# Sums of weights placed right behind the next pair's centroid products in a routed-attention and cosine-router kernel

## The chip, the cores and the metric

The kernel runs on one core of one Trainium2 chip. Its time is the device time of the whole program in microseconds (us), the median of several runs. Beside it stands one profiled execution, from which every duration of a part is read.

## The reference

The program computes two blocks one after the other. The first is an attention over clusters: queries and keys are assigned to the nearest of 16 centroids, and a query sees only keys of its own cluster. The second is a router with eight experts.

```python
q_assign = argmax(einsum('bhsd,hcd->bhsc', q_n, c_n), -1)   # B, H, S, D = 4, 8, 768, 64; 16 centroids
k_assign = argmax(einsum('bhsd,hcd->bhsc', k_n, c_n), -1)
mask = q_assign[:, :, :, None] == k_assign[:, :, None, :]
scores = where(mask, scale * q @ k.T, -1e9)
attn = softmax(scores)
x = (attn @ v) as (3072, 512)
logits = (x / |x|) @ (emb / |emb|).T / tau                  # 8 experts
e = argmax(logits); gate = softmax(logits)[e]
out = gate * (relu(x @ w1[e]) @ w2[e])                      # w1: 512 x 1024, w2: 1024 x 512
```

## The kernel before

**Pairs and turns.** The attention works on 16 pairs n = 0 to 15, each one batch and two heads. A pair has twelve units in two groups of six: a unit is one block of 128 keys against 384 queries of both heads. The main loop takes two units in one turn, so a pair has six turns, `it` = 0 to 5. The first group ends with turn 2, the second with turn 5. A place is written (pair, turn) here, and in the code's table `early` as (batch, pair of the batch, turn).

**The order is written by hand.** [...] In one turn the order is:

1. transfers of `load`: `v` of the next pair, `q` and `k` of the pair three further on (SP), and in eight pairs a megabyte of expert weights (ScalarE's queue);
2. `scores` of the next turn's two units: per unit four matrix products of the cluster numbers `hot` and four of q and k (L454) into `s_ps`, which has two buffers; `expo` (L465, ScalarE) turns them into `prob`, which has five;
3. `between(n, it)`, which holds everything that prepares the next pairs or serves the router, and the table `early` with the first part of the placement of tokens;
4. `attend` of this turn's two units: TensorE multiplies by `v` into `o_ps` (L476), which has one buffer; VectorE adds `prob` into `acc` (L485, L495). At a group's last unit ScalarE copies `o_ps` to `o_sb` (L500). The next group's first L476 must wait for that copy;
5. `unite` (GpSimd adds the halves of `o_sb`, L509), `divide` and `total`.

**Preparing a pair** (`prep_pieces`). `turn0` and `turn1` transpose q and k on VectorE (L356, `qT` and `kT`). `products` multiplies both by the centroids (L366, TensorE, into a `misc` buffer in PSUM, of which there are two), and VectorE transposes that to `asn` (L375). `choose` finds the best centroid on VectorE (L384 to L387: `amax`, `sel` twice, `pm`), writes it into `cd` on ScalarE (L389, L392), and SP transposes `cd` by a transfer into `hot` (L397), which the pair's first scores need, in turn 5 of the pair before.

**Finishing a pair.** `total` sums `acc` over the keys with products by ones (L523, TensorE, into `misc`); VectorE transposes these sums (L540) and takes their reciprocal (L541), GpSimd copies it eight times (L544). `divide` spreads it (L555, `den`) and multiplies (L559, `xT`). `rows` transposes `xT` (L576, `xb`) and SP writes it to `x_rows` in DRAM (four transfers).

**Routing a batch** (`route_pieces`), in the turns of the next batch. `products` multiplies `xT` by the experts (L598), `logits` transposes and adds (L611, L614), `choose` takes the best (L651 to L658), `read` fetches two blocks of `x_rows` back (SP, into `xr`), and `norms` squares and sums one block (L637, ScalarE). `pa.ranks`, `pa.firsts`, `pa.experts`, `pa.dest`, `pa.hot_blocks` and `pa.hot_rows` place the tokens of the first two batches.

**Experts.** After the last pair, 28 blocks of 128 tokens go through `turn_x` (the tokens transposed: by TensorE and an eviction for the first six, L958 and L961, by VectorE for the others, L951), `hidden` (L973, then L980) and `result` (L989, then L999 and L1000).

Of the kernel before, what the change touches and what calls it, by code (L numbers as in the profile page):

```python
# [39 lines left out]
def kernel(  # L40
# [12 lines left out]
    nc = tc.nc  # L53
# [23 lines left out]
    PIECES = KA + 2  # L77
# [77 lines left out]
    NP = len(pairs)  # L155
# [127 lines left out]
    def turned_experts():  # L283
        bk = misc()
        for c in range(KD):
            nc.tensor.transpose(
                bk[:, E * c : E * c + E], emb[:, P * c : P * c + P], ident[0:E, 0:E]
            )
        nc.vector.tensor_copy(
            embT[:, :, 0:E], bk[:, 0 : KD * E].rearrange("p (c e) -> p c e", e=E)  # L290
        )
# [278 lines left out]
    def rows(*gs):  # L570

        n, hq, _ = units[GU * gs[0]]
        b, hp = pairs[n]
        G = len(gs)
        xb = smp.tile([P, G * HS // SQ, SQ], F32, tag="xb", name="xb", bufs=2)
        nc.vector.transpose(  # L576
            xb.rearrange("p g i -> p (g i)"),
            xT[b, hp][:, hq : hq + G].rearrange("p k t -> p (k t)"),
        )
        t0 = S * b + HS * hq  # L580
        for c in range(P // SQ):
            c0 = P * c + SQ * hp
            nc.sync.dma_start(
                out=x_rows[t0 : t0 + G * HS, c0 : c0 + SQ].rearrange("(g t) i -> t g i", t=SQ),
                in_=xb[SQ * c : SQ * c + SQ],
            )
# [395 lines left out]
    def result(j, halves=(0, 1)):  # L982
# [30 lines left out]
    prepare, route = {}, {}  # L1013
    pa = Places(0, rta)
    early = {
        (2, 2, 0): pa.ranks,
        (2, 2, 4): pa.firsts,
        (2, 2, 5): pa.experts,
        (2, 3, 0): lambda: pa.dest(0),
# [13 lines left out]
    def piece(n, name, *args):  # L1033
        if n < NP:
            if n not in prepare:
                prepare[n] = prep_pieces(n)
            prepare[n][name](*args)

    def between(n, it):
        b, nb = divmod(n, NHP)  # L1040
        if n == 0:

            if it == 0:
                piece(1, "turn0")
                piece(1, "turn1")
            elif it == 1:
                piece(1, "products")
            elif it == 2:
                piece(1, "choose")
                turned_experts()  # L1050
        elif it == 0:
            piece(n + 1, "products")
        elif it == 1:
            piece(n + 1, "choose")
        elif it == 3:
            rows(2 * n - 2, 2 * n - 1)
        if it == 4:
            piece(n + 2, "turn0")
        elif it == 5:
            piece(n + 2, "turn1")  # L1060
        if b > 0:
            if nb == 0 and it == 3:
                route[b - 1] = route_pieces(b - 1)
            products, logits, read, norms, choose = route.get(b - 1, (None,) * 5)

            m = NJ * nb + it
            if m in (8, 11, 14):
                read((m - 8) // 3 * 2, (m - 8) // 3 * 2 + 2)
            if m in (11, 12, 14, 15, 17, 18):
                norms((11, 12, 14, 15, 17, 18).index(m))  # L1070
            if (nb, it) == (0, 4):
                products(0)
            elif (nb, it) == (0, 5):
                products(1)
            elif (nb, it) == (1, 2):
                logits(0)
            elif (nb, it) == (1, 3):
                logits(1)
            elif (nb, it) == (1, 4):
                choose()  # L1080
        if n == NP - 1 and it == 4:
            route[b] = route_pieces(b)
            route[b][2](0, NJ, 0, P - SQ)
        if b == B - 1 and (nb, it) == (3, 0):
            for j in range(2):
                weights1(j)
                weights2(j)
# [10 lines left out]
    with tc.manual_schedule(engines=by_hand):  # L1098
        begin()
        for i in range(0, len(units), 2):  # L1100
            n, it = divmod(i // 2, NJ)

            if n == it == 0:
                load(2, "qk")
            if it == 2 and n + 1 < NP:
                load(n + 1, "v")
            if it >= 4 and n + 3 < NP:
                load(n + 3, "qk"[it - 4])
            if it == 3 and n in (1, 2, 3, 5, 6, 7, 9, 10):

                slot, part = divmod(n - 1 - n // 4, 4)
                w, c, x = ((w1s, KD, moe_w1), (w2s, KF, moe_w2))[part // 2]
                cs = slice(c // 2 * (part % 2), c // 2 * (part % 2) + c // 2)
                nc.scalar.dma_start(
                    out=w[slot][:, cs], in_=x[0].rearrange("(c p) f -> p c f", p=P)[:, cs]
                )
            for m in range(i + 2, min(i + 4, len(units))):
                scores(m)
                expo(m)
            between(n, it)  # L1120
            if it == 4 and n == NP - 1:
                divide(2 * n)
            b, nb = divmod(n, NHP)
            if (b, nb, it) in early:
                early[b, nb, it]()
            if i + 2 == len(units):
                ats.close()
                tile_waits = {"side": "right", "reuse_waits": "tile"}
                psX = ctx.enter_context(tc.tile_pool(name="psX", bufs=1, space=PSUM, **tile_waits))
                turn_x(0, nc.scalar.copy, xp.tile([P, DM], F32, tag="acc", name="xTm", bufs=3))  # L1130
            for m in range(i, i + 2):
                attend(m)
            if it == 2:
                if n > 0:
                    divide(2 * n - 2, 2 * n - 1)
                unite(2 * n)
            elif it == 5:
                unite(2 * n + 1)
            if i + 2 == len(units):
                rows(ngroups - 2)  # L1140
                route[b][0](0)
            if it == 0 and n > 0:
                total(2 * n - 2, 2 * n - 1)
            elif it == 3 and n == NP - 1:
                total(2 * n)
        at.close()
        mop = ctx.enter_context(tc.tile_pool(name="mop", bufs=2, **tile_waits))
        rtb = ctx.enter_context(tc.tile_pool(name="rtb", bufs=1, **tile_waits))
        psH = ctx.enter_context(tc.tile_pool(name="psH", bufs=3, space=PSUM, **tile_waits))

        products, logits, read, norms, choose = route[B - 1]
        pb = Places(1, rtb)
        gates = gate_pieces(0, B - 1)
        gates[0]()
        hidden(0, (0,))
        order_x(3)
        total(ngroups - 1)
        divide(ngroups - 1)
        ato.close()
        psY = ctx.enter_context(tc.tile_pool(name="psY", bufs=2, space=PSUM, reuse_waits="tile"))  # L1160
        rows(ngroups - 1)
        gates[1]()
        gates[2]()
        hidden(0, (1,))
        gates[3]()
        weights1(2)
        turn_x(1, nc.scalar.copy)
        logits(0)
        read(0, NJ, P - SQ, P)
        products(1)  # L1170
        hidden(1, (0,))
        logits(1)
        choose()
        hidden(1, (1,))
        weights1(3)
        turn_x(2, nc.scalar.copy)
        pb.ranks()
        pb.firsts()
        for j in range(KA):
            fetch_gate(j)  # L1180
        result(0, (0,))
        pb.dest(0)
        pb.dest(1)
        pb.experts()
        result(0, (1,))
        weights2(2)
        pb.hot_blocks()
        pb.hot_rows(0, 1)
        hidden(2)
        weights1(4)  # L1190
        pb.tokens()
        fetch(4)
        fetch(5)
        for j in range(NJ):
            norms(j)
        gates = gate_pieces(B - 1, B)
        gates[0]()
        result(1, (0,))
        pb.pieces()
        fetch(6)  # L1200
        turn_x(3, nc.scalar.copy)
        for gate in gates[1:3]:
            gate()
        result(1, (1,))
        weights2(3)
        gates[3]()
        order_x(4)
        order_x(5)
        hidden(3)

        for j in range(2, usual):
            if 3 < j + 1 < usual:
                turn_x(j + 1, nc.vector.tensor_copy)
                if j + 4 < usual:
                    fetch(j + 4)
                hidden(j + 1)
                fetch_gate(j + 1)
            if 4 < j + 3 < usual:
                weights1(j + 3)
            result(j)  # L1220
            if 3 < j + 2 < usual:
                weights2(j + 2)

# [63 lines left out]
```

## Time and profile before

| | us |
|---|---|
| median of 3 runs | 758.27 |
| lowest and highest run | 758.07, 760.18 |
| the profiled execution | 759.15 |
| its span, first to last instruction | 757.4 |

The attention ends near 346 us of the span, where the first L973 starts; the rest is the experts' work. The profile page gives each engine's busy time and its share of the span, then groups of instructions: line, engine, operation, tiles, how often, then busy time and mean duration, then the idle time of the engine before them and what ended it. The list of waits gives, for an engine's line and what it waited for, the sum in us, the number of waits and the longest. The timeline gives start, duration and instruction, with the idle time before it in brackets. L12 is line 12 of the kernel before.

### The profile page before, as it was taken

How to read it: one execution, taken by the hardware profiler on the slowest of the kernel's cores; microseconds unless marked ns; L12 is line 12 of the kernel's file. 1: busy time of each engine (PE TensorE's matmuls, PEld its weight loads, DVE VectorE, ACT ScalarE, POOL GpSimd, SP SyncE). 2: the span in 40 equal slices, each digit the busy share in tenths (PEclk: the TensorE clock that was granted, in tenths of full speed). 3: DMA queues.
4: the chain of work that ended last, by engine and by line, in shares of the span. 5: the costliest groups of instructions: out<-in, count | busy, mean ns of one | idle time of the engine just before them, and what ended most of it. 6: DMA issues, size and time to landing. Idle time of an engine off the chain costs nothing. (4 is left out here: it accounts for less than half of the span.)

```text
span 757.4 us, 16422 instructions
## 1 busy us (share of the span) xinstructions
PE 734.9 (97%) x6670; PEld 442.7 (58%) x6670; DVE 328.2 (43%) x522; ACT 275.5 (36%) x438; POOL 253.6 (33%) x367
## 2 busy tenths in 40 slices
PE   7999999999988999999999999999999999999994
PEld 3444444444444444447766776776776776767762
DVE  5788887988769898987510100000000000000000
ACT  4666665766546555764150111111101111111110
POOL 2022222432121232460543453453453443543111
PEclk9999999999999999999999999999999999999998
DMA  9557876987578655487898865999767774147300
GB/s 147 86 115 152 164 124 134 196 163 146 91 165 183 109 95 97 109 268 169 283 367 319 301 238 186 337 331 332 245 236 249 261 252 147 49 148 253 122 15 24
DMA packets 246154, 140.26 MB, mean 185 GB/s; under 512 B 208177, under 2 KB 208177, under 8 KB 246076
## 3 DMA queue, kind: packets, MB, share of 16 engines
q1 hardware_dynamic: 236268, 117.09, 58.6%
q0 software_dynamic: 6432, 13.66, 5.0%
q10 hardware_dynamic: 3376, 8.44, 3.5%
q8 instruction: 54, 0.88, 0.5%
q14 instruction: 24, 0.20, 0.1%
HBM read 158.40 MB, written 13.64 MB: 227 GB/s over the span
## 5 line engine op out<-in xcount | busy, mean ns | idle before, releaser
L973 PEld LDWEIGHTS h_ps<-xTm,w1s 128*128 128x128 f32 x1792 | 204.3, 192 | 16.1 <-issue 12.7
L973 PE MATMUL h_ps<-xTm,w1s 128*128 128x128 f32 x1792 | 205.5, 275 | 2.2 <-DVE xTm L961 1.6
L989 PE MATMUL y_ps<-w2s,hT 128*128 128x512 f32 x448 | 197.0, 593 | 0.0
L465 ACT ACTIVATE prob<-s_ps 128x768 f32<-128x768 f32 x192 | 153.5, 812 | 95.2 <-PE s_ps L454 87.5
L454 PE MATMUL s_ps<-qT,kT 64*64 64x384 f32 x1536 | 156.0, 482 | 0.0
L476 PE MATMUL o_ps<-prob,v 64*64 64x385 f32 x1536 | 145.8, 493 | 5.3 <-ACT o_sb L500 3.3
L989 PEld LDWEIGHTS y_ps<-w2s,hT 128*128 128x128 f32 x448 | 83.0, 190 | 93.7 <-issue 93.7
L951 DVE STREAM_TRANSPOSE xTm<-xin 128x512 f32<-128x512 f32 x22 | 15.6, 711 | 272.9 <-remote 179.6
L495 DVE TENSOR_TENSOR acc<-acc,prob 128x768 f32<-128x768 f32 x128 | 123.7, 967 | 8.1
L980 ACT ACTIVATE hT<-h_ps 128x512 f32<-128x512 f32 x56 | 33.4, 597 | 203.9 <-PE h_ps L973 120.9
L476 PEld LDWEIGHTS o_ps<-prob,v 64*64 64x64 f32 x1536 | 56.9, 134 | 75.5 <-issue 58.3
L889 POOL DMA_INDIRECT xin<-x_rows,pidx x88 | 89.4, 1016 | 30.3 <-issue 28.1
L509 POOL TENSOR_TENSOR o_sum<-o_sb 128x385 f32<-128x385 f32 x30 | 32.2, 1073 | 156.8 <-ACT o_sb L500 156.7
L1000 POOL DMA_INDIRECT out_dram<-y,sidx x24 | 24.6, 1025 | 168.4 <-ACT y L999 162.5
L454 PEld LDWEIGHTS s_ps<-qT,kT 64*64 64x64 f32 x1536 | 56.1, 133 | 38.7 <-issue 35.6
L454 PE MATMUL s_ps<-hot 64*64 64x384 bf16 x768 | 64.7, 325 | 1.8 <-DVE hot L415 1.0
L999 ACT ACTIVATE y<-y_ps,gatein 128x512 f32<-128x512 f32 x28 | 19.2, 687 | 129.4 <-PE y_ps L989 123.2
L544 POOL COPY inv<-inv 32x12 f32<-32x12 f32 x120 | 43.9, 365 | 52.8 <-DVE inv L541 48.5
L454 PEld LDWEIGHTS <-hot 64*64 64x64 bf16 x768 | 23.3, 107 | 38.2 <-issue 36.9
L485 DVE SCALAR_TENSOR_TENSOR acc<-prob,prob 128x768 f32<-128x768 f32 x32 | 31.3, 979 | 0.0
L889 POOL DMA_INDIRECT gatein<-gate_rows,gidx x28 | 28.3, 1010 | 8.9 <-issue 8.9
L500 ACT COPY o_sb<-o_ps 128x770 f32<-128x770 f32 x32 | 25.5, 798 | 14.9 <-PE o_ps L476 14.3
(201 smaller groups left out, 359.1 us busy)
## 6 DMA issues: line engine op xcount, KB each, us to landing
w1s<-in_moe_w_dram SPq DMA_DIRECT2D x28, 2048.0 KB
w2s<-in_moe_w_dram SPq DMA_DIRECT2D x28, 2048.0 KB
v<-in_v_dram SPq DMA_DIRECT2D x128, 48.0 KB
q<-in_q_dram SPq DMA_DIRECT2D x60, 96.0 KB
k<-in_k_dram SPq DMA_DIRECT2D x60, 96.0 KB
x_rows<-xb SPq DMA_DIRECT2D x60, 96.0 KB
xr<-x_rows SPq DMA_DIRECT2D x9, 512.0 KB
w1s<-in_moe_w_dram ACTq DMA_DIRECT2D x4, 1024.0 KB
```

The costliest lines, as they stand in the source:

```text
L454: nc.tensor.matmul(s_ps[D * half : D * half + D, h, 0:HS], lhsT=l[rows, half], rhs=r[rows], start=part == (1 if len(parts) < 2 else 0), st ...
L465: nc.scalar.activation(d["prob"][:, :, 0:HS], d["s_ps"][:, :, 0:HS], ACTF.Exp, scale=scale)
L476: nc.tensor.matmul(g["o_ps"][D * h : D * h + D, half, 0:HE], lhsT=ld[n]["v"][keys, j, h], rhs=d["prob"][keys, h, 0:HE], start=(j == 0), st ...
L485: nc.vector.scalar_tensor_tensor(out=g["acc"], in0=un[i - 1]["prob"][:, :, 0:HS], scalar=NJ * EPS, in1=d["prob"][:, :, 0:HS], op0=ALU.add, ...
L495: nc.vector.tensor_tensor(g["acc"], g["acc"], d["prob"][:, :, 0:HS], ALU.add)
L500: nc.scalar.copy(t["o_sb"], g["o_ps"][:, :, 0:HE])
L509: add(t["o_sum"][:, hq], t["o_sb"][:, 0], t["o_sb"][:, 1], ALU.add)
L544: nc.gpsimd.tensor_copy(inv2[M * to : M * to + M, :, i % 2], inv[M * i : M * i + M])
L889: nc.gpsimd.indirect_dma_start(out=to, out_offset=None, in_=of, in_offset=bass.IndirectOffsetOnAxis(ap=at, axis=0), bounds_check=n - 1, oo ...
L973: nc.tensor.matmul(bk[:, m : m + P], lhsT=w1s[j % 2][:, c, f0 + m : f0 + m + P], rhs=d["xT"][:, P * c : P * c + P], start=(c == 0), stop=( ...
L980: nc.scalar.activation(d["hT"][:, f0 : f0 + 512], bk, ACTF.Relu)
L989: nc.tensor.matmul(bk, lhsT=d["hT"][:, P * c : P * c + P], rhs=w2s[j % 2][:, c], start=(c == 0), stop=(c == KF - 1),)
```

## The change

Five things move; no instruction of the computation is added or dropped.

- `turn0` of the pair after next goes from turn 4 to turn 5, `turn1` from turn 5 to turn 0 of the next pair, `products` from turn 0 to 1, `choose` from turn 1 to 2, `rows` from turn 3 to 4, `divide` from turn 2 to 3, the load of `v` from turn 2 to 0, the weights' transfer from turn 3 to 4. In the last pair `rows`, `divide` and `total` stay.
- `total` of the pair before goes from the end of turn 0 to the middle of turn 1, right behind `products`.
- The router's products, logits and choosing come one turn later; the reads go out in turns 9, 13 and 15 of a batch (before: 8, 11, 14), and the norms come in turns 15, 16, 18, 19, 21, 22 (before: 11, 12, 14, 15, 17, 18).
- `pa.ranks` goes from turn 0 to turn 3 of pair 10.
- Among the experts, `turn_x(1)` comes right behind the last `total`, `turn_x(2)` between the halves of `hidden(1)`, and `turn_x(4)` and `turn_x(5)` between the halves of a result instead of right ahead of the `hidden` that uses them.

```diff
-        (2, 2, 0): pa.ranks,
+        (2, 2, 3): pa.ranks,
...
-        elif it == 0:
-            piece(n + 1, "products")
-        elif it == 1:
-            piece(n + 1, "choose")
-        elif it == 3:
-            rows(2 * n - 2, 2 * n - 1)
-        if it == 4:
+        else:
+            if it == 0:
+                piece(n + 1, "turn1")
+            elif it == 1:
+
+                piece(n + 1, "products")
+                if n + 1 < NP:
+                    total(2 * n - 2, 2 * n - 1)
+            elif it == 2:
+                piece(n + 1, "choose")
+            if it == (4 if n + 1 < NP else 3):
+                rows(2 * n - 2, 2 * n - 1)
+        if it == 5:
             piece(n + 2, "turn0")
-        elif it == 5:
-            piece(n + 2, "turn1")
...
-            if m in (8, 11, 14):
-                read((m - 8) // 3 * 2, (m - 8) // 3 * 2 + 2)
-            if m in (11, 12, 14, 15, 17, 18):
-                norms((11, 12, 14, 15, 17, 18).index(m))
-            if (nb, it) == (0, 4):
+            if m in (9, 13, 15):
+                third = (9, 13, 15).index(m)
+                read(2 * third, 2 * third + 2)
+            if m in (15, 16, 18, 19, 21, 22):
+                norms((15, 16, 18, 19, 21, 22).index(m))
+            if (nb, it) == (0, 5):
                 products(0)
-            elif (nb, it) == (0, 5):
+            elif (nb, it) == (1, 0):
                 products(1)
-            elif (nb, it) == (1, 2):
+            elif (nb, it) == (1, 3):
                 logits(0)
-            elif (nb, it) == (1, 3):
+            elif (nb, it) == (1, 4):
                 logits(1)
-            elif (nb, it) == (1, 4):
+            elif (nb, it) == (1, 5):
                 choose()
...
-            if it == 2 and n + 1 < NP:
+            if it == (0 if n else 2) and n + 1 < NP:
                 load(n + 1, "v")
...
-            if it == 3 and n in (1, 2, 3, 5, 6, 7, 9, 10):
+            if it == 4 and n in (1, 2, 3, 5, 6, 7, 9, 10):
...
+            if n > 0 and it == (3 if n + 1 < NP else 2):
+                divide(2 * n - 2, 2 * n - 1)
             if it == 2:
-                if n > 0:
-                    divide(2 * n - 2, 2 * n - 1)
                 unite(2 * n)
...
-            if it == 0 and n > 0:
+            if it == 0 and n == NP - 1:
                 total(2 * n - 2, 2 * n - 1)
...
         total(ngroups - 1)
+        turn_x(1, nc.scalar.copy)
...
-        turn_x(1, nc.scalar.copy)
...
         choose()
+        turn_x(2, nc.scalar.copy)
         hidden(1, (1,))
         weights1(3)
-        turn_x(2, nc.scalar.copy)
...
             if 3 < j + 1 < usual:
-                turn_x(j + 1, nc.vector.tensor_copy)
+                if j + 1 >= PIECES:
+                    turn_x(j + 1, nc.vector.tensor_copy)
...
-            result(j)
+            result(j, (0,))
+
+            if 3 < j + 2 < PIECES:
+                turn_x(j + 2, nc.vector.tensor_copy)
+            result(j, (1,))
```

## The prediction

> **What bounds the kernel now.** I read four views in this order: the page's busy shares, the waits of TensorE, the timeline around the two slices where TensorE dips, and the timeline of an undisturbed pair.
>
> ```profile
> PE 734.9 (97%) x6670; PEld 442.7 (58%) x6670; DVE 328.2 (43%) x522; ACT 275.5 (36%) x438; POOL 253.6 (33%) x367
> ...
> L476 PE MATMUL o_ps<-prob,v 64*64 64x385 f32 x1536 | 145.8, 493 | 5.3 <-ACT o_sb L500 3.3
> ```
>
> TensorE is the bound; something moves the end only if it shortens TensorE's own stream or a wait in it. Its waits:
>
> ```profile
> PE o_ps L476 <- ACT o_sb L500: 3.3, 2, 2.8
> ...
> PE h_ps L973 <- DVE xTm L961: 1.6, 2, 0.8
> ...
> PE h_ps L973 <- ACT xTm L961: 0.6, 1, 0.6
> ...
> ACT junk L637 <- DMA xr<-x_rows: 10.2, 5, 4.1
> ```
>
> The last line says why the first exists. The norms (L637) stand in ScalarE's queue ahead of the copy of `o_sb` (L500), and `o_ps` has one buffer, so the next group's L476 waits for that copy:
>
> ```profile
> 221.37 0.63 ACT L637 ACTIVATE junk<-xr 128x512 f32<-128x512 f32 x1 [4.14 <-DMA xr<-x_rows]
> ...
> 222.00 0.78 ACT L500 COPY o_sb<-o_ps 128x770 f32<-128x770 f32 x1
> ...
> 222.84 3.15 PE L476 MATMUL o_ps<-prob,v 64*64 64x385 f32 x16 [2.77 <-ACT o_sb L500]
> ```
>
> L476 took 3.15 us here and 1.46 in other turns: after 2.77 us of idleness the clock was halved. The same happens at 246 us (2.02 us idle); an idle stretch of about 0.6 us at 158 us halved nothing.
>
> An undisturbed pair (pair 2, turn 0):
>
> ```profile
> 57.11 0.52 PE L366 MATMUL misc<-qT,cnB 128*32 128x384 f32 x2
> ...
> 57.89 1.52 PE L476 MATMUL o_ps<-prob,v 64*64 64x385 f32 x16
> 58.03 0.58 DVE L375 STREAM_TRANSPOSE asn<-misc 128x384 f32<-128x384 f32 x1 [0.73 <-PE misc L366]
> ...
> 59.35 0.88 PE L523 MATMUL misc<-acc,ones 128*32 128x192 f32 x16
> 60.16 0.36 PE L454 MATMUL s_ps<-hot 64*64 64x384 bf16 x4
> ...
> 60.32 0.58 DVE L540 STREAM_TRANSPOSE sums<-misc 128x384 f32<-128x384 f32 x1 [0.87 <-PE misc L523]
> ```
>
> I took the start of L476 in every turn. A plain turn is 2.91 us, everywhere. A turn with the centroid products (L366) is 0.88 longer, one with the sums (L523) 0.99: a pair is 6 x 2.91 + 1.87 = 19.33. VectorE works 17.7 of these and idles 1.6 (0.73 + 0.87, the two brackets).
>
> [...] neighbouring groups of four start 0.31 to 0.33 us apart within a mode, 0.41 where 64x64 turns into 128x32 or back. [...] the slowed stretches here are 3.4 us each and cost about 1.7. [...]
>
> **The change part by part.**
>
> (a) Sums behind products, pairs 1 to 14 (pair 15 keeps its place). Both are 128x32[...]. Adding the gaps anew (0.41 in, 0.35, 0.33, 0.55 through the sums' groups, 0.26 out, less the 0.31 that a turn has anyway, plus 0.06 of slower first groups) gives 1.65 instead of 1.87: **-0.22 x 14 = -3.1** (ends 0.10 and 0.35: -1.4, -4.9).
>
> (b) Norms three or more turns later behind their reads. They now come five or six turns behind, over 14 us, where a read took 3.7 to 6.6 us from issue to landing, and never in turns 2 and 5, which end with an `o_sb` copy. The disturbed turns were 6.83, 5.64, 5.88, 5.83 (pairs 10, 11) where products, sums and ranks explain 15.8 of 24.2: -8.4; pair 7 gave 0.9 away, pair 6 0.1. At (12,1) another 0.56 went to sums that waited for VectorE, busy with the early ranks work; these sums now come a turn later. **-10.0** (ends -6, if later runs stall less; -10.5).
>
> (c) All else one turn later: `kT`, products, choose, divide, rows. VectorE's order becomes asn, sums, inv, two acc, amax, sel, sel, pm. ScalarE's becomes: the turn's two exponentials, the `cd` writes (L389, L392), and in the *same* turn 2 the `o_sb` copy. Before, choosing was in turn 1, which ends with no copy. This is the new wait. Pair 0 already runs so (without sums) and prices it:
>
> ```profile
> 26.60 0.55 DVE L387 TENSOR_REDUCE pm<-sel 128x24 bf16<-128x384 bf16 x1
> ...
> 27.18 0.41 ACT L389 ACTIVATE cd<-pm,wcd 128x24 bf16<-128x24 bf16 x1 [0.68 <-DVE pm L387]
> ...
> 27.41 0.61 ACT L392 ACTIVATE cd<-pm 64x24 bf16<-64x24 bf16 x2
> 28.05 0.80 ACT L500 COPY o_sb<-o_ps 128x770 f32<-128x770 f32 x1
> ...
> 28.90 1.52 PE L476 MATMUL o_ps<-prob,v 64*64 64x385 f32 x16
> ```
>
> From the start of pm to turn 3's L476: 2.30 us. Now let P be the start of L366 in turn 1. asn starts at P + 0.92 (57.11 to 58.03). The sums' last group starts at about P + 1.25, and L540 follows 0.42 behind (as in pair 2): P + 1.67. inv 0.62 later, acc after 0.14, then acc, amax, sel, sel, pm at pair 0's and pair 2's spacings (1.02, 0.88, 0.53, 0.60, 0.39): pm at P + 5.85, L476 of turn 3 at P + 8.15. Without the wait it would be P + 1.51 (L476 of turn 1) + 2 x 2.91 + 0.04 = P + 7.37. So TensorE waits **0.78 in each of 14 pairs: +10.9** (ends 0.5 and 1.1 per pair: 7 and 15). It is too short to halve the clock, by the 0.6 us case. The cover that is gone: before, the copy ended about 0.4 us ahead of its user. Queued behind `cd` are also the next two exponentials; they end at P + 8.9 and 9.7, and turn 4's scores want their buffers at P + 9.4 and 10.3: no second stall.
>
> In that wait TensorE does what stands ahead of L476 in turn 3 for nothing: logits of pairs 5, 9, 13 (0.57 each before) and ranks of pair 10 (0.4): **-2.0**.
>
> VectorE does not fall behind: 17.7 + 0.25 against 19.9. Only pair 10 piles up ranks, firsts, experts and dest (3.1 us) and brings pair 11's asn late: **+0.5** (0 to 1.5).
>
> Queues. SP: the transposition of `cd` (L397) now goes out at pm + 1.48 (pair 0), and by the trace's landings it landed 3.7 to 4.2 us later in all fifteen pairs; turn 5's L454 wants it 6.5 after pm: 0.8 to 1.3 us to spare, in pair 0 1.1. `v` (eight issues, some 4.3 us) now goes ahead of it instead of behind, `rows` (four) and the q and k loads (eight) behind; the `v` buffer is free by then, and its issues end five us before L397. The weights' transfer from ScalarE's queue (6 to 7.8 us) starts a turn later and is over by then. Taken as 0; a landing 1 us late in the eight pairs with weights would cost up to 4. POOL: eight inv copies (0.365 each) end near P + 5.3, den reads them at P + 9.3: 0.
>
> (d) The expert stage: `turn_x` 4 and 5 move between the halves of a result, `turn_x(1)` ahead of a hidden half. The instructions stay; the three waits (0.78, 0.78, 0.63) fall under 3.5 to 3.8 us of products: **-2.2** (-1.5 to -2.4). `turn_x(2)` had no wait: 0.
>
> Sum: -3.1 - 10.0 + 10.9 - 2.0 + 0.5 - 2.2 = **-5.9**. The profiled execution took 759.15 (span 757.4), 0.9 over the median of 758.27, within the runs' own spread of 2.1; against the median: **752.4**.
>
> **Rivals.**
>
> 1. As summed: the wait moves from norms to `cd`, net gain. 0.60, 749 to 756.
>
> 2. No new wait, because VectorE gets pm out 0.8 us earlier than reckoned (pair 2's brackets show it idle there): the 8.9 net of (c) goes, **743.5**. Against it: pair 0 had 0.09 us of stall even without sums. 0.10.
>
> 3. The new wait decides. The other parts give 14.8 (3.1 + 10.0 + 2.2 - 0.5), so from 1.2 us per pair (14 x 1.2 - 2.0) the kernel loses. Should VectorE still have acc work ahead of asn, pm comes up to 1 us later: 1.78 x 14 - 2.0 - 14.8 = +8, **766**. For it: VectorE idles only 0.73 us before asn now. Against: its load per pair has 1.9 us of room in the longer pair. Milder forms end at 757 to 762. 0.23.
>
> 4. The norms still wait, because reads queue on SP behind `v`, q and k: most of the 10 stays, some **761**. Against: SP sat idle 1.4 to 9.7 us before L397 in every pair, and norms have twice the distance. 0.07.
>
> **Numbers.** No change is taken as within 0.3% (2.3 us), about what a measurement of this kernel can tell. Case 1 is faster in 0.55 of its 0.60, case 2 always; of cases 3 and 4, 0.09 lies within 0.3%, 0.05 is faster, 0.16 slower. Together: faster 0.70, same 0.14, slower 0.16. Range 747 to 759.5, from a wait of about 0.4 to one of 1.3 us per pair.
>
> **What would show it.** Right: L476 in turn 3 waits for `o_sb` about 0.8 us in pairs 1 to 14, ScalarE waits for pm at L389; L523 starts about 0.33 us behind the last L366; no wait of L637 on `xr`; no half clock between 220 and 250; no wait of L973 on `xTm`. Wrong: turn 3 at 2.91 (case 2), turn 3 above 4.1 us or L454 waiting for `hot` (case 3), L637 waiting on `xr` (case 4).

## The result and the profile after

| | us |
|---|---|
| after: median of 4 runs (lowest to highest) | 779.75 (774.57 to 784.30) |
| before, on the same chip: median of 4 runs | 759.12 (758.07 to 760.18) |
| ratio after to before, 95% interval | 1.027 (1.0202 to 1.0337) |
| after: profiled execution, its span | 779.24, 777.5 |

The change makes the kernel slower by 20.6 us. The forecast was 752.4, and the range ended at 759.5. By stages of the two traces: the attention (first L476 to first L973) went from 327.6 to 348.9 us, the experts (first L973 to the start of the last L989) from 401.0 to 398.1. The loss lies in the attention alone. In experiments 5 and 6 below, one run each, over 1.5% above the fastest of its kernel, is left out.

The page of the kernel after, busy shares and two groups of L476 and L454 (busy us and mean ns of one; behind the second bar the idle time ahead of the group and what ended it). L476 and L454 keep their line numbers; the weights' transfer moves from L1114 to L1120:

```profile
PE 738.5 (95%) x6670; PEld 448.4 (58%) x6670; DVE 330.5 (43%) x522; ACT 275.5 (35%) x438; POOL 262.7 (34%) x367
...
L476 PE MATMUL o_ps<-prob,v 64*64 64x385 f32 x1536 | 144.8, 493 | 6.7 <-ACT o_sb L500 6.6
...
L454 PE MATMUL s_ps<-hot 64*64 64x384 bf16 x768 | 66.4, 330 | 20.3 <-DMA hot<-cd 18.5
```

TensorE's busy time rose by 3.6 us only (734.9 to 738.5); the rest is idleness. The waits of TensorE after (sum in us, number, longest):

```profile
PE s_ps L454 <- DMA hot<-cd: 18.5, 9, 3.3
PE o_ps L476 <- ACT o_sb L500: 6.6, 13, 0.7
```

The second line is the wait that the prediction forecast: short, in 13 pairs. The first did not exist before. The idleness is not all that it costs: in three places, at such waits, the granted clock stood at 0.50 for 3.4 us (at 102, 170 and 263 us). Summed over the turns in which it falls, beyond a plain turn of 2.91 us and its other work, `hot` costs about 25 us.

The timeline of the kernel after shows how, in pair 1 (start, duration, instruction; in brackets the idle time before it):

```profile
48.77 0.41 ACT L389 ACTIVATE cd<-pm,wcd 128x24 bf16<-128x24 bf16 x1 [0.94 <-DVE pm L387]
48.99 0.61 ACT L392 ACTIVATE cd<-pm 64x24 bf16<-64x24 bf16 x2
49.03 0.82 PE L454 MATMUL s_ps<-qT,kT 64*64 64x384 f32 x8
49.63 1.45 SPq L397 DMA_TRANSPOSE hot<-cd  x1
49.63 0.80 ACT L500 COPY o_sb<-o_ps 128x770 f32<-128x770 f32 x1
49.93 0.41 ACTq L1120 DMA_DIRECT2D w1s<-in_moe_w_dram  x1
50.32 1.52 ACT L465 ACTIVATE prob<-s_ps 128x768 f32<-128x768 f32 x2
...
50.48 1.52 PE L476 MATMUL o_ps<-prob,v 64*64 64x385 f32 x16 [0.63 <-ACT o_sb L500]
...
56.48 0.36 PE L454 MATMUL s_ps<-hot 64*64 64x384 bf16 x4 [1.57 <-DMA hot<-cd]
```

Read it from the bottom. L454 of turn 5 waited 1.57 us for the transposition issued at 49.63, which landed at 56.44, 6.81 us later. A megabyte of weights was issued 0.30 us behind it, at 49.93. The two exponentials at 50.32 stand ahead of L1120 in ScalarE's program, yet the transfer went out 0.39 us before them. The six operations of ScalarE in this list ran in the order in which the program has them; the transfer did not keep its place among them.

The same places in pair 1 of the kernel before:

```profile
44.73 2.38 SPq L397 DMA_TRANSPOSE hot<-cd  x1
...
46.97 0.80 ACT L500 COPY o_sb<-o_ps 128x770 f32<-128x770 f32 x1 [0.54 <-PE o_ps L476]
47.00 0.40 ACTq L1114 DMA_DIRECT2D w1s<-in_moe_w_dram  x1
...
52.49 0.33 PE L454 MATMUL s_ps<-hot 64*64 64x384 bf16 x4
```

The weights come 2.27 us behind L397, and the scores want `hot` only 7.76 us behind it.

Landing times of `hot`, from the issue of L397 until the trace has the last of its completion signals, before and after:

| | before | after |
|---|---|---|
| the eight pairs with a weights' transfer (1, 2, 3, 5, 6, 7, 9, 10) | 3.7 to 4.2 us | 6.8 to 8.7 us |
| pairs 0, 4, 11, 12, 13 | 3.7 to 4.2 us | 3.7 to 4.7 us |
| pair 8 | 3.7 to 4.2 us | 5.6 us |
| weights issued behind L397 (those eight pairs) | 2.3 to 2.9 us | 0.3 to 0.4 us |
| from L397 to the use of `hot`, where nothing is late | 7.7 to 9.0 us (pair 0: 5.1) | 5.1 us (pair 4) |

### The profile page after: what moved, and what is told of

Same layout as the page of the kernel before. It is cut to its first block, busy times and chain, and to the rows that moved or that the text cites. A ratio compares the mean times of both kernels' runs of the same rounds, so it can differ in the third digit from the quotient of the medians.

```text
span 777.5 us, 16428 instructions
## 1 busy us (share of the span) xinstructions
PE 738.5 (95%) x6670; PEld 448.4 (58%) x6670; DVE 330.5 (43%) x522; ACT 275.5 (35%) x438; POOL 262.7 (34%) x367
## 5 line engine op out<-in xcount | busy, mean ns | idle before, releaser
L973 PEld LDWEIGHTS h_ps<-xTm,w1s 128*128 128x128 f32 x1792 | 204.5, 192 | 13.7 <-issue 13.1
L973 PE MATMUL h_ps<-xTm,w1s 128*128 128x128 f32 x1792 | 205.1, 275 | 0.0
L989 PE MATMUL y_ps<-w2s,hT 128*128 128x512 f32 x448 | 197.3, 592 | 0.0
L454 PE MATMUL s_ps<-qT,kT 64*64 64x384 f32 x1536 | 160.7, 494 | 0.0
L476 PE MATMUL o_ps<-prob,v 64*64 64x385 f32 x1536 | 144.8, 493 | 6.7 <-ACT o_sb L500 6.6
L989 PEld LDWEIGHTS y_ps<-w2s,hT 128*128 128x128 f32 x448 | 82.8, 190 | 92.8 <-issue 92.8
L476 PEld LDWEIGHTS o_ps<-prob,v 64*64 64x64 f32 x1536 | 56.7, 134 | 75.9 <-issue 56.8
L454 PE MATMUL s_ps<-hot 64*64 64x384 bf16 x768 | 66.4, 330 | 20.3 <-DMA hot<-cd 18.5
L509 POOL TENSOR_TENSOR o_sum<-o_sb 128x385 f32<-128x385 f32 x30 | 34.4, 1147 | 146.5 <-ACT o_sb L500 146.5
L454 PEld LDWEIGHTS s_ps<-qT,kT 64*64 64x64 f32 x1536 | 58.6, 136 | 39.8 <-issue 37.0
L544 POOL COPY inv<-inv 32x12 f32<-32x12 f32 x120 | 49.9, 416 | 73.1 <-DVE inv L541 68.7
L454 PEld LDWEIGHTS <-hot 64*64 64x64 bf16 x768 | 24.3, 108 | 59.1 <-issue 34.0
L485 DVE SCALAR_TENSOR_TENSOR acc<-prob,prob 128x768 f32<-128x768 f32 x32 | 34.7, 1086 | 2.8 <-ACT prob L465 2.8
L375 DVE STREAM_TRANSPOSE asn<-misc 128x384 f32<-128x384 f32 x16 | 9.3, 582 | 53.1 <-PE misc L366 53.1
```

The costliest lines, as they stand in the source:

```text
L454: nc.tensor.matmul(s_ps[D * half : D * half + D, h, 0:HS], lhsT=l[rows, half], rhs=r[rows], start=part == (1 if len(parts) < 2 else 0), st ...
L476: nc.tensor.matmul(g["o_ps"][D * h : D * h + D, half, 0:HE], lhsT=ld[n]["v"][keys, j, h], rhs=d["prob"][keys, h, 0:HE], start=(j == 0), st ...
L485: nc.vector.scalar_tensor_tensor(out=g["acc"], in0=un[i - 1]["prob"][:, :, 0:HS], scalar=NJ * EPS, in1=d["prob"][:, :, 0:HS], op0=ALU.add, ...
L509: add(t["o_sum"][:, hq], t["o_sb"][:, 0], t["o_sb"][:, 1], ALU.add)
L544: nc.gpsimd.tensor_copy(inv2[M * to : M * to + M, :, i % 2], inv[M * i : M * i + M])
L973: nc.tensor.matmul(bk[:, m : m + P], lhsT=w1s[j % 2][:, c, f0 + m : f0 + m + P], rhs=d["xT"][:, P * c : P * c + P], start=(c == 0), stop=( ...
```

## Experiments

Ratios are to runs of the kernel before on the same chip, whose medians there were 760.1 to 760.7. Two theories stood at the outset. **A**: the weights' transfer, now issued 0.3 us behind the transposition, stretches it beyond the slack that the shift of a turn has left. **B**: other transfers do it (`v` ahead of L397, q, k and `rows` behind), or choosing in turn 2 by itself. The first four experiments tell them apart and take out the second, small wait; the others ask what the parts of the change are worth alone.

**1. Weights one turn later.** On the kernel after:

```diff
-            if it == 4 and n in (1, 2, 3, 5, 6, 7, 9, 10):
+            if it == 5 and n in (1, 2, 3, 5, 6, 7, 9, 10):
```

> The changed kernel with one edit: the weights' megabyte (ScalarE's queue) goes out in turn 5 instead of turn 4. Theory A (the weights are issued 0.3 us behind the transposition of cd[...], so hot lands 6.8 to 8.7 us after its issue and the scores of turn 5 wait): hot lands 3.7 to 4.7 us after its issue in every pair, the 18.5 us of L454 waiting for hot and the half-clock stretches behind them go, turn 5 and the turn after lose about 25 us over the pairs, time about 755; the o_sb wait of 0.81 per pair stays. Rival B (hot is late because v, q and k now stand otherwise around it in SP's queue): hot as late as before, time stays at 775 to 784.

Measured: 758.55 (756.41 to 761.08, 20 runs), ratio 0.9973 (0.9957 to 0.9988). One line takes back 21 us. TensorE's waits in it:

```profile
PE o_ps L476 <- ACT o_sb L500: 6.9, 13, 0.9
PE s_ps L454 <- DMA hot<-cd: 3.6, 3, 2.4
```

`hot` lands after 3.7 to 4.6 us again, but for three pairs (6, 8 and 10: 6.6, 5.7, 4.8). Their turns still lose 5.9 us, which more than makes up the 3.5 us over the 755 expected. A holds, and B falls as the main cause: everything else of the change is still there. The wait on `o_sb` stays, as it should. In pairs 6 and 10 L397 went out 1.0 and 1.3 us late, right behind a read of `x_rows` on SP.

**2. Weights in turn 2 of the kernel before.** Here the transfers meet with nothing else moved:

```diff
-            if it == 3 and n in (1, 2, 3, 5, 6, 7, 9, 10):
+            if it == 2 and n in (1, 2, 3, 5, 6, 7, 9, 10):
```

> The kernel before with one edit: the weights in turn 2, which puts their issue next to that of the transposition to hot (turn 1), and nothing else of the change. Theory A (the meeting alone makes hot late): hot lands 6 to 9 us after its issue in the eight pairs with weights, 3.7 to 4.2 in the others; the scores wait less than in the changed kernel, since choosing one turn earlier leaves 4 us to spare: 0 to 5 us per pair, 765 to 785. Rival B (lateness comes from where v, q and k stand): hot lands 3.7 to 4.2 us after its issue everywhere, time as before.

Measured: 757.28 (one run). From its timeline, pair 1:

```profile
43.86 0.40 ACTq L1114 DMA_DIRECT2D w1s<-in_moe_w_dram  x1
...
44.71 2.47 SPq L397 DMA_TRANSPOSE hot<-cd  x1
```

The weights are issued 0.85 us ahead of L397, and `hot` lands at 52.03, 7.32 us later. It is so in exactly the eight pairs with weights, 6.3 to 8.3 us, against 3.7 to 4.7 in the others. The latency is as A expects; the cost that it was expected to bring is not there, for L454 hardly waits on `hot` (once, 0.02 us, in pair 10, where it lands just as it is wanted): choosing in turn 1 leaves about 8 us until the use. So in this one execution the meeting alone is harmless, and it takes the second half of the change, the shorter slack, to turn it into a loss.

**3. The second wait taken away, weights left where they are.** ScalarE's writes of `cd` and L397 go behind the copy of `o_sb`:

```diff
             nc.vector.tensor_reduce(pm, sel, axis=AXX, op=ALU.max)
-            pm = pm.rearrange("p (s h) -> p s h", h=2)
+            t["pm"] = pm
+            if n < 2:
+                numbers()
+
+        def numbers():
+            pm = t["pm"].rearrange("p (s h) -> p s h", h=2)
...
                 attend(m)
+            if n > 0 and it == 2:
+                piece(n + 1, "numbers")
```

> The changed kernel with one edit: ScalarE's writes of cd and the transposition to hot come behind the o_sb copy of turn 2 (VectorE's part of choosing stays where it is). Theory A (two waits in a row, the later one decides in pairs with weights): the 0.81 us of turn 3 goes in all 14 pairs, but where the weights make hot late the same 0.8 comes back in turn 5, so only the six pairs without weights gain: about 5 us, 775. Rival C (the two waits add up, hot's landing moves ahead with the rest): 11 us, 768.5.

Measured: 787.61 (786.86 to 788.61, 4 runs), ratio 1.0368 (1.0331 to 1.0405), 8 us above the kernel after instead of below. In this kernel L460 is the old L454:

```profile
PE s_ps L460 <- DMA hot<-cd: 28.7, 10, 4.3
```

No wait of L476 on `o_sb` is left, so that wait is indeed made by the `cd` writes ahead of the copy. But without it TensorE reaches turn 5 0.8 us earlier, while `hot` is issued no earlier and still takes 6.9 to 8.9 us in the eight pairs with weights: the wait on `hot` grows by 10 us, and eight stretches at half clock follow instead of three (the mean granted clock is 0.978 against 0.987). My expectation forgot that a stall ahead of a deadline also moves the deadline.

**4. Both.** Experiments 1 and 3 together:

> Both edits: weights in turn 5, cd and hot behind the o_sb copy. Theory A: neither turn 3 nor turn 5 waits, every pair without routing is 6 x 2.91 + 1.6 + 0.1, time 743 to 745. Rival: hot now lands at most 0.4 us ahead of its use, so turn 5 waits some tenths per pair: 746 to 750.

Measured: 756.90 (754.50 to 762.64, 18 runs), ratio 0.9965 (0.9948 to 0.9981); some 12 us of the gain were missing. A plain pair takes 19.17 to 19.21 us, as expected (19.33 before), but `hot` has no slack at all: in pair 1 it lands at 54.00 and is used at 54.04, and where a transfer is a little late TensorE waits at once (5.9 us in five waits). With choosing in turn 2, either TensorE waits for the copy or `hot` comes at the last moment.

**5. The same with later reads** (turns 9, 15, 16 of a batch), to keep reads away from L397:

```diff
-            if m in (9, 13, 15):
-                third = (9, 13, 15).index(m)
+            if m in (9, 15, 16):
+                third = (9, 15, 16).index(m)
```

> As w5_split, and the second and third read of a batch go out in turns 15 and 16 instead of 13 and 15, so that none stands ahead of the transposition to hot in SP's queue. Theory (in pairs 6 and 10 of w5_split that read held the transposition back until SP was free, and it then landed 4.9 to 5.7 us later): hot of these pairs lands in time to 0.3 us, 3 to 6 us less than w5_split, 751 to 754. Rival (hot is simply too close to its use everywhere after the shift by one turn): 755 to 757.

Measured: 757.21 (752.91 to 761.20, 12 runs), ratio 0.9943 (0.9918 to 0.9967). Not better; the waits on `hot` are 9.0 us in six. The reads of pairs 6 and 10 were not the only thing in the way, and the time is just above the rival's 755 to 757.

**6. The norms alone, on the kernel before:**

```diff
-            if m in (8, 11, 14):
-                read((m - 8) // 3 * 2, (m - 8) // 3 * 2 + 2)
-            if m in (11, 12, 14, 15, 17, 18):
-                norms((11, 12, 14, 15, 17, 18).index(m))
+            if m in (9, 13, 15):
+                third = (9, 13, 15).index(m)
+                read(2 * third, 2 * third + 2)
+            if m in (15, 16, 18, 19, 21, 22):
+                norms((15, 16, 18, 19, 21, 22).index(m))
```

> The kernel before with one part of the change: reads in turns 9, 13, 15 of a batch and norms in turns 15, 16, 18, 19, 21, 22. Theory (the prediction's part b): no wait of L637 on xr, no half clock at 220 and 250 us, the turns of pairs 10 and 11 at 3.8 and 3.9: 9 to 10 us less, about 749.5. Rival (the o_sb copies are held by something else that came last by accident, or reads go out late behind v, q and k): less than 3 us.

Measured: 759.35 (750.78 to 762.03, 19 runs), ratio 0.9976 (0.9949 to 1.0003): no gain in the median. Five runs lie at 750.8 to 753.2, near the forecast, the others at 757.2 and more. In the profiled execution (762.03, the slowest of these) the wait for `xr` is gone, and pairs 9 and 10 take 20.8 and 21.2 us instead of 23.6 and 23.2. What was won is lost at another place. Its timeline ahead of pair 8's scores, SP's queue and ScalarE's:

```profile
165.00 2.24 SPq L182 DMA_DIRECT2D k<-in_k_dram  x4
...
167.35 1.84 SPq L397 DMA_TRANSPOSE hot<-cd  x1
...
167.54 0.41 ACTq L1115 DMA_DIRECT2D w1s<-in_moe_w_dram  x1
...
180.64 0.54 PE L454 MATMUL s_ps<-hot 64*64 64x384 bf16 x4 [7.44 <-DMA hot<-cd]
```

The new read stands with `v`, `rows`, q and k in SP's queue, which hands L397 out 0.11 us behind the last k, in turn 2 instead of turn 1. There it meets the weights, 0.19 us apart, and lands after 13.24 us: 7.4 us of waiting and two stretches at half clock (L454 behind the wait took 0.54 us instead of 0.33; the mean granted clock is 0.989). It is the loss of the kernel after in a kernel without its other parts.

**7. Norms, the experts' part, and weights in turn 4, on the kernel before** (the diff of experiment 6, the change's `turn_x` lines, and):

```diff
-            if it == 3 and n in (1, 2, 3, 5, 6, 7, 9, 10):
+            if it == 4 and n in (1, 2, 3, 5, 6, 7, 9, 10):
```

> The kernel before with three parts of the change: reads and norms in the later turns, the experts' turn_x moved, and the weights in turn 4. Choosing stays in turn 1, so the transposition to hot goes out some 8 us ahead of the weights. Theory A (what cost b_norms its gain is the same meeting of hot and weights: there hot of pair 8 went out late and took 13 us to land): hot lands within 5 us of its issue, no wait on it above 0.5 us, pairs 10 and 11 at 19.3 to 19.8, time 747 to 749. Rival D (the reads' traffic itself holds hot back): hot waits of 5 us and more stay, 755 or more.

Measured: 748.72 (748.16 to 749.57, 4 runs), ratio 0.9836 (0.9789 to 0.9884). The same place in its timeline:

```profile
165.81 2.15 SPq L397 DMA_TRANSPOSE hot<-cd  x1
...
168.57 0.40 ACTq L1115 DMA_DIRECT2D w1s<-in_moe_w_dram  x1
```

L397 is late on SP here too, and as close behind the same k loads (0.11 us), but the weights come 2.76 us behind it, and `hot` lands after 3.95 us; so it was not the k loads alone that made it late in experiment 6. In no pair does it take over 4.3 us, L454 never waits for it, and the clock is never halved in the attention (the mean granted clock of the whole execution is 0.997). The weights are not 8 us behind L397, as expected, but 2.8 to 5.3. The attention takes 319.7 us (327.6 before), the experts 398.1.

**8. The sums alone, on the kernel before:** `total` right behind `products`, both in turn 0.

```diff
         elif it == 0:
             piece(n + 1, "products")
+            if n + 1 < NP:
+                total(2 * n - 2, 2 * n - 1)
...
-            if it == 0 and n > 0:
+            if it == 0 and n == NP - 1:
                 total(2 * n - 2, 2 * n - 1)
```

> The kernel before with one part of the change: the sums right behind the centroid products, both in turn 0 as the products were. Theory ([...] the prediction's part a): turn 0 at 4.5, turn 1 at 2.96, 0.2 to 0.3 us per pair, 3 to 4 us in all; no wait of turn 3 on o_sb, since choosing stays in turn 1, where no copy stands behind it. Rival: the sums now come before VectorE has the last acc ready (it idles only 0.73 us ahead of asn), TensorE waits for it, 0 or slower.

Measured: 756.87 (754.03 to 760.55, 20 runs), ratio 0.9952 (0.9933 to 0.9970). Undisturbed pairs take 19.08 us instead of 19.33. The groups of its timeline follow without a gap:

```profile
59.99 0.49 PE L366 MATMUL misc<-kT,cnB 128*32 128x384 f32 x2
60.30 0.87 PE L523 MATMUL misc<-acc,ones 128*32 128x192 f32 x16
61.10 1.52 PE L476 MATMUL o_ps<-prob,v 64*64 64x385 f32 x16
```

In three pairs where VectorE is behind with the router's work the sums wait for `acc` (3.7 us in all).

**9. All the parts without the shift of a turn:** experiments 7 and 8 together.

> As b_norms_w4, and the sums right behind the products in turn 0: all that the change gains without its shift by one turn. Theory: the gains add up, 743 to 746. Rival (VectorE, now the busiest beside TensorE, makes sums or products wait in the pairs with routing): not better than b_norms_w4.

Measured: 751.99 (751.03 to 752.57, 4 runs), ratio 0.9875 (0.9827 to 0.9922), worse than experiment 7 alone:

```profile
PE misc L523 <- DVE acc L495: 5.3, 5, 1.8
```

In turn 0 the sums come too early for five pairs (6, 10, 11, 12, 14), and cost there more than they bring elsewhere.

**10. The same, with the sums of those five pairs left at the end of turn 0:**

```diff
+            if n not in (6, 10, 11, 12, 14, 15):
+                total(2 * n - 2, 2 * n - 1)
...
-            if it == 0 and n > 0:
+            if it == 0 and n in (6, 10, 11, 12, 14, 15):
```

> As b_all, but in pairs 6, 10, 11, 12 and 14, where b_all's sums waited for VectorE's last acc, the sums stay at the end of turn 0; in the nine others they come right behind the products. Theory [...]: no wait of L523 on acc, 9 x 0.25 = 2.3 us below b_norms_w4, 746 to 747. Rival [...]: 748.5 or more.

Measured: 748.57 (746.63 to 756.28, 6 runs), ratio 0.9854 (0.9808 to 0.9900). The waits on `acc` are gone, but it can't be told from experiment 7. In the profiled execution L397 of pair 7 was late again, the weights followed 1.8 us behind it, and it landed after 8.82 us, with a wait of 3.0. Pairs without trouble take 19.08.

**The distance decides.** Time from L397 to the weights' issue, and what `hot` took:

| where | weights behind L397 | landing |
|---|---|---|
| experiment 2, eight pairs | -0.85 us | 6.3 to 8.3 us |
| experiment 3, eight pairs | -0.1 to 0.1 us | 6.9 to 8.9 us |
| experiment 6, pair 7 | 0.19 us | 13.2 us |
| after, eight pairs | 0.3 to 0.4 us | 6.8 to 8.7 us |
| experiment 6, pair 10 | 1.1 us | 8.4 us |
| experiment 5, pair 7 | 1.7 us | 4.8 us |
| experiment 10, pair 7 | 1.8 us | 8.8 us |
| before, eight pairs | 2.3 to 2.9 us | 3.7 to 4.2 us |
| experiment 7, pair 7 | 2.76 us | 3.95 us |
| experiment 1, pair 6, with a read of `x_rows` issued 0.54 us ahead of L397 | 3.1 us | 6.6 us |

Two rows are exceptions. In experiment 5 the weights are close, yet `hot` takes only 4.8 us. In the last row they are as far off as they should be, and another transfer stands close ahead. Over all twelve traces: where the weights were issued from 0.85 us ahead of L397 to 1.8 us behind it, 27 of 28 landings took 6.3 us or more; where they came 2.2 to 5.4 us behind, 60 of 68 took 3.6 to 4.7 us and eight 4.8 to 6.6. So in these traces the meeting decides whether `hot` takes 4 us or 7, and something else can add a smaller delay.

## Why the prediction was wrong

**The step that failed** is the paragraph "Queues" in part (c): "The weights' transfer from ScalarE's queue (6 to 7.8 us) starts a turn later and is over by then. Taken as 0". Two things were wrong in it.

First the instant. "A turn later" is not set against L397, which moved too. In its new place L1120 stands behind turn 3's exponentials, but the queue did not wait for those to run: the transfer went out 0.3 us behind L397, where before there were 2.3. In pair 1 L1120 went out at 49.93 and the exponentials ahead of it began at 50.32. What it did follow can be read too: in all eight pairs L1120 comes 0.07 to 0.2 us behind the last product of L454 that the second of them reads (in pair 1 that ends at 49.85), and in all eight of the kernel before L1114 comes 0.15 us behind the last L476 that the copy ahead of it reads. From these figures I estimate that the transfer waited for the inputs of the operation ahead of it, not for its run; then its new instant could have been reckoned from the trace before. No run varies this by itself, and in pairs 1 to 3 of experiment 7 the weights come 1.0 to 1.6 us behind those inputs.

Second the price. I had measured the slack at 0.8 to 1.3 us (pair 4 shows 1.26), and put a transfer that comes 1 us late at up to 4 us in all. It came 3.0 to 4.9 us later than the usual 3.8, in eight pairs. The packets show it: the transposition is 1536 packets of 256 bytes, moved from 45.91 to 48.15 us before, when the first weights' packet came at 48.16; after, from 50.81 to 55.75 us (its last completion signal came at 56.44), with packets of the weights among them from 51.18 to 54.81. In those 3.63 us only 379 of the 1536 started, against 273 in the 0.37 us ahead of them and 884 in the 0.94 us behind. The windows view of the kernel after, at the bad stretch and at pair 4's (window, length, then busy us of PE, PEld, DVE, ACT, POOL with counts, clock, DMA share, GB/s):

```profile
49.60:56.50 6.90, 4.70 (x64) 2.01 (x60) 6.62 (x8) 3.84 (x6) 1.68 (x1) 1.00 0.90 234
117.60:121.50 3.90, 3.27 (x48) 1.57 (x48) 3.75 (x5) 2.84 (x5) 1.68 (x1) 1.00 0.70 128
```

The DMA engines have more to do in the first (0.90 of their time against 0.70), and move more bytes (234 GB/s against 128). From 51.5 to 54.5 us 16.0 packets were under way on average, 1.3 of them the transposition's; before, from 46 to 48 us, 19.1 of 19.3 were. So by the packets `hot` is late while the engines move bytes that nobody waits for yet; how the engines choose among the packets was not shown.

**Part by part.**

- (a) Sums behind products: right. Turn 1 is 1.57 us over a plain one and turn 2 0.05, together 1.62 where I had 1.65: -0.25 per pair, -3.5 instead of -3.1. Experiment 8 gives the same -0.25. In the traces L523 starts 0.41 us behind the last of L476 before, where 64x64 turns into 128x32, and 0.30 behind the last of L366 after, where both are 128x32; what makes the longer distance was not shown.
- (b) Norms: the mechanism right, the size a little over. Experiment 7 has the attention 8.0 us shorter, where the parts of (b) that lie in the norms were put at 9.4. It is only reached when `hot` is left alone: experiment 6, without that, got none of it in the median.
- (c) The wait for `o_sb`: right. Turn 3 is 0.81 us longer in pairs 1 to 13 and 0.32 in pair 14, 10.9 us in all, as forecast to the tenth (0.78 each; in pair 1 pm starts 5.85 us behind L366, the figure forecast). The first of the two logits of pairs 5, 9 and 13 vanish under it, and with waits of at most 0.7 us it never halved the clock.
- (c) Queues: forecast 0, measured about +25.
- (d) Experts: -2.8 (401.0 to 398.1), forecast -2.2; no wait of L973 on `xTm` is left.

Without `hot`, -3.5 - 8.0 + 10.9 - 2.0 + 0.5 - 2.8 gives -4.9 (-2.0 and +0.5 are the forecast's own figures, and -8.0 is from experiment 7); with 25 more it is +20.1, and the profiled execution moved by 779.24 - 759.15 = 20.1. That it agrees so closely is luck: the start of the kernel, ahead of the first L476, was 1.6 us longer in this execution (18.7 and 20.3), as it varies between executions of every kernel here (18.7 to 21.4). Within some 2 us the forecast of -5.9 was right for everything but one transfer. Experiment 1 agrees: it is 1.5 us under the kernel before, with 5.9 us still lost to a late `hot`.

Of the signs that I had named, "L454 waiting for `hot`" came true. I had put it under rival 3, as the price of a late pm; but pm came on time (L397 at pm + 1.45, forecast 1.48), so that rival's mechanism did not occur either. None of the four rivals was a meeting of two transfers.

**Open.** Seventeen landings of 4.8 to 6.6 us, without weights from 0.9 us ahead to 2 us behind (pair 8 of the kernel after, single pairs of experiments 1, 3, 4, 5, 6 and 8), have no cause that a run shows. Some follow a read of `x_rows` by half a microsecond, which is argued, not tried by itself. Eleven of them have a packet of 16 KB of the queue that the profile page calls "instruction" (q8) starting 2 to 4 us behind L397; so have only 14 of the other 134 landings without such weights. That is a second suspect, not a cause shown. Nor is it shown why the runs of experiment 6 fall into two groups. L397 of pair 7 is late on SP in all four traces of the kernel before with the later reads (2.6 to 4.1 us behind pm in experiments 6, 7, 9 and 10, against 1.4 to 1.7 without them), but how close it then comes to the weights differs (0.2 to 3.1 us).

## What to carry to other kernels

When a step moves, list every transfer that it issues or that is issued near it, with the time between the issues and the slack until the use, both from the trace, and multiply a late landing by the pairs in which it can happen: here a slack of some 4 us forgave, in one execution, the same meeting that cost 25 us with a slack of 1.2. Place a transfer on a compute engine's queue by when the trace shows it issued, not by the end of the operations ahead of it; in the kernels before and after it went out within 0.2 us of the last input of the operation ahead. A gain that depends on a transfer's landing was safest here with the large, unhurried transfer at least some 2.3 us behind the small, urgent one (3.7 to 4.2 us to land in the kernel before): the norms and the experts' part with the weights in turn 4 give 748.7, 1.6% under the kernel before, with none of the shift.

## What the hardware showed unexpectedly

- A transposition that took 3.7 to 4.2 us in the kernel before took 6.3 to 8.9, and 13.2 once, where a 1 MB transfer was issued from 0.85 us ahead of it to 1.8 us behind it (27 of 28 cases); at 2.2 us behind and more it took 3.6 to 4.7 in 60 of 68, and at most 6.6.
- ScalarE's queue sent a transfer out 0.4 us before two exponentials that stand ahead of it in the program had begun, 0.08 us behind the product that the second of them reads.
- The length of an idle stretch did not alone decide whether TensorE's clock was halved. In the kernel after, thirteen waits of 0.2 to 0.7 us never halved it; waits on `hot` of 2.1, 2.1 and 2.8 us did (to 0.50, for 3.4 us each time), and others of 2.2, 2.8 and 3.3 us did not.
